# Attention and two feed-forward layers on one core: layer 1's outputs grouped in DRAM, and the refill of the weight slots rescheduled

## The chip, the cores and the metric

The kernel runs on one core of a Trainium2 chip. Its time is the device time of one execution, in microseconds (us); three executions of the kernel before took 1013.91, 1014.51 and 1015.23 us, so the median is 1014.51 us. Less is better.

## The reference

Inputs are float32, the four weight matrices float64.

```python
local = softmax(causal(q @ k.T / 8)) @ v           # 4 batches, 8 heads, 576 rows, 64 columns
mem   = (phi(q) @ M_prev) / (phi(q) @ z_prev)       # phi(x) = x + 1 above 0, exp(x) below
x     = sigmoid(beta) * mem + (1 - sigmoid(beta)) * local     # laid out as 2304 tokens x 512
h = x @ w_in;  x = g1(h) @ w_out                   # layer 1: 512 -> 2048 -> 512
h = x @ w_in2; y = leaky(h, 0.01) @ w_out2         # layer 2, the same sizes
```

`g1(h)` is h above 1, 0 below -1, and (h+1)^2/4 between. Each float32 product is done as three products of a high and a low part, so weights and activations are split in two before TensorE uses them.

## The kernel before

The first 211 us are attention with the first weights; the change leaves them alone. After that come four parts of 36 steps each: layer 1's first half of the 2048 hidden columns (part 0), its second half (part 1), and the same for layer 2 (parts 2 and 3). Tokens go in chunks of 256, nine in all, in groups `(0,1) (2,3) (4,5) (6,7) (8,)`: a pair takes 8 steps, one for each block f of 128 hidden columns, and the single chunk 4 steps with two blocks in each. A step is one run of h (the first product, 12 matmuls of 512 columns for a pair) and one run of Y (the second product) of a block three steps older. Parts 2 and 3 do Y with seven products in place of eight, from sums and differences of weights. h has one PSUM bank only: TensorE can start the next h when ScalarE has copied the last one out.

A part needs 16 weight halves of 512 KB: `in0` to `in7` for h and `o0` to `o7` for Y, each with one slot in SBUF, and in parts 2 and 3 also `ex0` to `ex3` (768 KB, sums for two o halves). They come as float64 bit patterns and are decoded: one ScalarE instruction (L613), five on VectorE (L615 to L623), then the split (L638 and L639).

For parts 1 to 3 the halves are decoded during the part before, each about two steps after the one before (`COUNTS`, L607, 16 in a part's 36 steps), stored to `w_d` in DRAM (L641; the sums to `ex_d`, L678 and L680), and read back into the slots at the part's start. `renew` (L698) issues all these reads, as soon as a slot is free by the plan: `in0` and `in1` four steps before the part's first step, then two a step, the o slots from one step before it on (fetches at L702).

Layer 1's outputs go through DRAM too: part 0 stores sums (`yp_d`), part 1 loads them (`pp`, L876), adds them (L886) and stores y (`y_d`, L880); parts 2 and 3 read y as x (L730). Each of these tiles holds one chunk, so a pair's half of the columns goes in four transfers of 128 KB. Layer 2 keeps its sums in `op_d` with two transfers of 256 KB a chunk, and writes `out` likewise (L955, loads at L848).

The order of every engine's instructions is fixed ahead by a planner (`Plan.order`). Each task has an engine, a cost, a priority in steps, its predecessors and its buffers ("rooms"); the planner plays the engines forward in time and always takes the ready task of lowest priority value. For a DMA it counts 0.6 us on the issuing queue and a constant landing time (`lag`, 4.6 us for the float64 loads, 5.2 for the fetches), whatever else is moving. On the chip every engine then runs its list in order and waits where the data isn't there. All DMAs of the four parts are issued from SyncE's queue (SP), in order.

Of the kernel before, what the change touches and what calls it, by code (L numbers as in the profile page):

```python
# [8 lines left out]
F32 = mybir.dt.float32  # L9
# [124 lines left out]
def attn_moe_moe_kernel(ctx, tc, q, k, v, m_prev, z_prev, beta, w1i, w1o, w2i, w2o, out):  # L134
# [97 lines left out]
    yp_d = [dram.tile([128, 4, TC], F32, name=f"yp_d{c}") for c in range(NCH)]  # L232
    y_d = [dram.tile([128, 4, TC], F32, name=f"y_d{c}") for c in range(NCH)]
    op_d = [{c: dram.tile([128, 2, DM], F32, name=f"op_d{m}_{c}") for c in ([NCH - 1] if m == 0 else range(NCH))} for m in range(2)]
# [372 lines left out]
    PER, AHEAD, DELAY, COUNTS = 36, 3, 4, (17, 17, 14)  # L607
# [76 lines left out]
    HALVES = [(f, 0) for f in range(NSLOT)] + [(f, 1) for f in range(NSLOT)]  # L684

    def weights(seg, k, prio, after, kept, halves):

        f, x = HALVES[k]
        parts = decode(seg, f, x, prio, after)
        if x == 0 or not SEVEN[seg]:  # L690
            kept[f, x] = [keep_half(seg, f, x, *parts, prio)[1]]
            return
        halves.append(parts)
        if f % 2:
            kept[f, x] = kept[f - 1, x] = keep_out(seg, f // 2, *zip(*halves), prio)
            halves.clear()

    def renew(seg, kept):  # L698
        base = PER * seg

        def fetch(room, src, after):
            return steps.add("SP", SEND, prio - 1.5, after, [room], lambda: nc.sync.dma_start(out=as_r(at(room)), in_=src), lag=5.2)  # L702

        for f, x in HALVES:
            free = f // 2 - (1 if x else 4)
            prio, after = base + free - 0.4, [*kept[f, x], mm_at[base + min(free, 0) - 1]]
            room = Room(f"o{f}" if x else f"in{f}")
            ready = fetch(room, w_d[seg][f, x], after)
            if x == 0 or not SEVEN[seg]:
                half_room[seg, f, x], half_ready[seg, f, x] = room, ready  # L710
                continue
            out_room.setdefault((seg, f // 2), []).append(room)
            out_ready.setdefault((seg, f // 2), []).append(ready)
            if f % 2:
                ex = Room(f"ex{f // 2}")
                out_room[seg, f // 2].append(ex)
                out_ready[seg, f // 2].append(fetch(ex, ex_d[seg][f // 2], after))

    def load_x(seg, group, prio):

        room, ready = Room("x"), []
        for j, c in enumerate(group):
            raw = Room("xraw")

            def load(c=c, raw=raw):
                xf = staging(at(raw))
                if SEGS[seg][0] == 0:
                    load_chunk(c, xf)
                else:
                    nc.sync.dma_start(out=xf, in_=y_d[c])  # L730

            after = stored_y.get((seg, c), []) if SEGS[seg][0] else []
# [112 lines left out]
    def load_kept(pp, keep, rows):  # L845
        for i in range(2):
            o = at(pp)[:, i]
            nc.sync.dma_start(out=o.rearrange("p a t -> p (a t)") if rows else o, in_=keep[i])  # L848
# [10 lines left out]
    def finish_plain(seg, group, banks, lhs, after, step):  # L859
        half, pair, n, add = SEGS[seg][1], len(group) == 2, group[0], steps.add  # L860
        for i, lh in enumerate(lhs):
# [3 lines left out]

            t = add("ACT", 2 * from_psum(512), step - 2, after, [*banks.rooms, lh], copies)

            def places(d, i=i):

                if pair:  # L870
                    return [(k, j, d[n + j][:, 2 * i + k]) for k in range(2) for j in range(2)]
                return [(k, None, d[n][:, 2 * k:2 * k + 2]) for k in range(2)]

            def load(pp, places=places):
                for k, j, d in places(yp_d):
                    nc.sync.dma_start(out=at(pp)[:, k] if j is None else at(pp)[:, k, j], in_=d)  # L876

            def store(lh=lh, places=places):
                for k, j, d in places(y_d if half else yp_d):
                    nc.sync.dma_start(out=d, in_=at(lh)[k] if j is None else at(lh)[k][:, j])  # L880

            ts = [t]
            if half:
                pp = Room("pp")
                before = add("SP", 4 * SEND, step - 2, [stored_y[seg - 1, n, i]], [pp], lambda pp=pp, load=load: load(pp), lag=4.0)
# [8 lines left out]
    def finish(seg, group, j, banks, y3, lhs, after, step):  # L894

        layer, half = SEGS[seg][:2]
        pair, n = len(group) == 2, group[0]
        rows = layer == 1 or not pair
        c = n + j
        s, lh, add, tt = Room("s"), lhs[j], steps.add, vec.tensor_tensor  # L900

        def cols(d, i):
            return d[n + i].rearrange("p (b j) t -> p j b t", j=2)[:, j]

        if rows:
            keep = [op_d[layer][c][:, i] for i in range(2)]
        else:
            keep = [cols(yp_d, i) for i in range(2)]
        if half and layer:
            goal = [out[TC * c + 128 * i:TC * c + 128 * i + 128] for i in range(2)]  # L910
        elif half and not rows:
            goal = [cols(y_d, i) for i in range(2)]
        else:
            goal = keep
# [5 lines left out]
        def sums_a():  # L920
            (s0, s1), (lo, hi) = at(s), at(lh)
# [6 lines left out]
        def sums_b():  # L928
            (s0, s1), (lo, hi) = at(s), at(lh)
            tt(lo[:, 1], s1[:, 0], s1[:, 1], ALU.add)  # L930
            tt(lo[:, 0], s1[:, 0], lo[:, 0], ALU.subtract)
# [8 lines left out]
        if half and rows and not layer:  # L940
            return turn_single(lh, t, banks, step)
        if half:
            pp = Room("pp")

            before = add("SP", 2 * SEND, step - 1, [stored_y[seg - 1, c, 0]] if rows else [stored_y[seg - 1, n, i] for i in range(2)], [pp],
                         lambda: load_kept(pp, keep, rows), lag=4.0)
            ts = [add("DVE", dve(512), step, [t, before], [lh, pp], lambda i=i: vec.tensor_tensor(
                at(lh)[i], at(lh)[i], at(pp)[:, i], ALU.add), lag=SLACK) for i in range(2)]
        else:
            ts = [t, t]  # L950

        def store():
            for i in (1, 0):
                o = at(lh)[i]
                nc.sync.dma_start(out=goal[i], in_=o.rearrange("p a t -> p (a t)") if rows else o)  # L955

        t = add("SP", 2 * SEND, step + 0.2, ts, [lh], store, lag=3.0)
        if rows:
            stored_y[seg, c, 0] = stored_y[seg, c, 1] = t
        else:  # L960
            stored_y[seg, n, j] = t
        if half and not layer:
            for i in range(2):
                stored_y.setdefault((seg + 1, n + i), []).append(t)

    def turn_single(lh, t, used, step):

        n, banks, res, pp, add = NCH - 1, Room(used.kind), Room("lh"), Room("pp"), steps.add

        def turn():  # L970
            for i in range(2):
                x = at(lh)[i].rearrange("p a t -> p (a t)")
                for et in range(4):
                    pe.transpose(at(banks)[et // 2][:, et % 2, 128 * i:128 * i + 128], x[:, 128 * et:128 * et + 128], ident)

        def load():
            for i in range(2):
                nc.sync.dma_start(out=at(pp)[:, i], in_=yp_d[n][:, 2 * i:2 * i + 2])

        def store():  # L980
            for i in range(2):
                nc.sync.dma_start(out=y_d[n][:, 2 * i:2 * i + 2], in_=at(res)[i])

        before = add("SP", 2 * SEND, step - 1, [stored_y[0, n, i] for i in range(1)], [pp], load, lag=4.0)
        t = add("PE", 900, step + 1.2, [t], [lh, banks], turn)
        ts = [add("DVE", dve(512), step - 1, [t, before], [banks, res, pp], lambda i=i: vec.tensor_tensor(
            at(res)[i], at(banks)[i], at(pp)[:, i], ALU.add)) for i in range(2)]
        t = add("SP", 2 * SEND, step + 2, ts, [res], store, lag=3.0)
        stored_y.setdefault((2, n), []).append(t)
# [10 lines left out]
    def plan_steps():  # L1000
        step, queue, ready_x, used = 0, [], None, "Yb"
        whens = [PER * (seg + i / n) for seg, n in enumerate(COUNTS) for i in range(n)]
        decodes = [(when, 1 + k // 16, k % 16) for k, when in enumerate(whens)]
        kept, halves = {seg: {} for seg in range(1, 4)}, []
        groups = [(seg, g) for seg in range(4) for g in GROUPS]

        def pop(step):
            seg, group, p, j, gg, ready, banks, (y3, lhs) = queue.pop(0)
            pair, layer = len(group) == 2, SEGS[seg][0]
            if (seg, group) == groups[-1] and p >= NSLOT // 2 - 2:  # L1010
                last_parts.append((p, gg, banks, y3))
                if not last_pp:
                    last_pp.append(Room("pp"))
                    keep = [op_d[1][NCH - 1][:, i] for i in range(2)]
                    steps.add("SP", 2 * SEND, step - 2, [stored_y[2, NCH - 1, 0]], [last_pp[0]], lambda: load_kept(last_pp[0], keep, True))
# [17 lines left out]
        for i, (seg, group) in enumerate(groups):  # L1033
# [12 lines left out]
            for p in range(NSLOT // 2):  # L1046
                gg = Room("gg") if pair or p % 2 == 0 else gg
                g, all_ready = (Room("ga"), Room("gb")), []
                for f in ((2 * p, 2 * p + 1) if pair else (2 * p,)):
# [20 lines left out]
                    while decodes and decodes[0][0] - AHEAD <= step:  # L1070
                        when, n, k = decodes.pop(0)
                        weights(n, k, when + DELAY, [mm], kept[n], halves)
# [4 lines left out]
                    if f == 2 and i + 1 < len(groups):  # L1077
                        ready_x = load_x(*groups[i + 1], step + 1)
# [5 lines left out]
            if i % 5 == 4 and seg < 3:  # L1084
                renew(seg + 1, kept[seg + 1])
# [106 lines left out]
```

## Time and profile before

| | |
|---|---|
| median of three runs | 1014.51 us |
| profiled execution, its own time | 1012.95 us |
| span in the profile | 1011.1 us |
| TensorE busy | 983.5 us (97%) |
| VectorE busy | 719.0 us (71%) |
| ScalarE busy | 596.7 us (59%) |
| DMA moved | 164.36 MB |

In the rows, PE is TensorE, PEld its weight load, DVE VectorE, ACT ScalarE, SP the queue that issues the DMAs. PEclk 1.00 is 2.4 GHz granted, 0.50 is 1.2 GHz. L641 is line 641 of the kernel. A bracket at the end of a row is the idle time before the instruction and what ended it.

### The profile page before, as it was taken

The page shows a single profiled execution, that of the slowest core. Times are in us where ns is not written, and L with a number is a line of the kernel's source. Part 1 is how long each engine was busy: PE and PEld are TensorE (multiplying, and loading weights), DVE is VectorE, ACT ScalarE, POOL GpSimd, SP SyncE. Part 2 cuts the span into 40 slices and gives each one's busy share as a digit, 9 for nine tenths or more (in the row PEclk, how much of TensorE's full clock was granted, in tenths as well). Part 3 has the DMA queues.
Part 4 walks back from the last instruction along what each step waited for, and adds up shares of the span by engine and source line. Part 5 has one row for each costly group of instructions (what it writes and reads, how often), then busy time and mean ns, then how long its engine had stood idle before and what let it go on. Part 6 is the DMA issues. An engine that isn't in the chain of part 4 may idle for free.

```text
span 1011.1 us, 19985 instructions
## 1 busy us (share of the span) xinstructions
PE 983.5 (97%) x7794; PEld 865.7 (86%) x7794; DVE 719.0 (71%) x1571; ACT 596.7 (59%) x1056; POOL 50.7 (5%) x78
## 2 busy tenths in 40 slices
PE   8999999999999999899999998899999999999997
PEld 6888888888888888788888897799999999999997
DVE  7999987758675666556766565697888874665646
ACT  7899888866565666555556563364454643443433
POOL 1332221100000000000000000000000000000000
PEclk9999999999999999999999999899999999999999
DMA  9666743133644339945353589654332993212203
GB/s 195 166 151 151 181 115 91 46 113 111 196 147 168 130 140 310 334 133 185 121 198 135 198 300 391 221 176 151 142 132 100 306 394 94 84 35 70 70 15 104
DMA packets 141661, 164.36 MB, mean 163 GB/s; under 512 B 70016, under 2 KB 110208, under 8 KB 141568
## 3 DMA queue, kind: packets, MB, share of 16 engines
q1 hardware_dynamic: 139696, 162.44, 49.9%
q8 instruction: 61, 1.00, 0.4%
q10 hardware_dynamic: 1872, 0.66, 0.3%
q14 instruction: 32, 0.26, 0.1%
HBM read 108.02 MB, written 55.05 MB: 161 GB/s over the span
## 4 chain that ended last, share of the span: by engine, by line
PE 74%; DVE 11%; DMA 9%; ACT 4%; issue 2%; SPq 0%; DVEq 0%; ACTq 0%
PE h L744 12%; PE h L745 12%; PE h L746 12%; PE Y L746 11%; PE Y L745 11%; PE Y L744 11%; DVE e L395 4%; DMA w_d<-raw 2%; ACT e L400 2%; PE W L291 2%; DMA i<-w_d 2%; DMA raw<-in_moe_w_in_dram 1%; PE W L430 1%; DMA q<-in_q_dram 1%; DMA raw<-y_d 1%
## 5 line engine op out<-in xcount | busy, mean ns | idle before, releaser
L744 PE MATMUL h<-ffn_x,i 128*128 128x512 f32 (+1 forms) x312 | 116.7, 374 | 8.0 <-ACT ga L798 6.2
L744 PE MATMUL h<-xh,i 128*128 128x512 f32 (+1 forms) x320 | 119.1, 372 | 3.2 <-ACT gb L802 3.2
L745 PE MATMUL h<-xl,i 128*128 128x512 f32 (+1 forms) x320 | 118.8, 371 | 0.0
L746 PE MATMUL h<-xh,i 128*128 128x512 f32 (+1 forms) x320 | 118.2, 370 | 0.0
L745 PE MATMUL Y<-gl,o 128*128 128x512 f32 (+1 forms) x320 | 117.8, 368 | 0.0
L744 PE MATMUL Y<-gh,o 128*128 128x512 f32 (+1 forms) x320 | 117.8, 368 | 0.0
L746 PE MATMUL Y<-gh,o 128*128 128x512 f32 (+1 forms) x320 | 117.7, 368 | 0.0
L745 PE MATMUL h<-ffn_x,i 128*128 128x512 f32 (+1 forms) x312 | 116.2, 372 | 0.0
L746 PE MATMUL h<-ffn_x,i 128*128 128x512 f32 (+1 forms) x312 | 115.9, 371 | 0.0
L801 ACT ACTIVATE r<-h 128x512 f32<-128x512 f32 x70 | 41.9, 599 | 116.7 <-PE h L746 116.7
L745 PE MATMUL Y<-o,gh 128*128 128x256 f32 x288 | 81.5, 283 | 0.0
L746 PE MATMUL Y<-o,gl 128*128 128x256 f32 x288 | 81.5, 283 | 0.0
L744 PE MATMUL Y<-o,gh 128*128 128x256 f32 x288 | 81.3, 282 | 0.0
L400 ACT ACTIVATE e<-e,mx 128x384 f32<-128x384 f32 (+4 forms) x144 | 71.7, 576 | 15.8 <-DVE mx L395 15.7
L744 PEld LDWEIGHTS h<-ffn_x,i 128*128 128x128 f32 x312 | 59.5, 191 | 17.9 <-ACT ga L798 6.8
L744 PEld LDWEIGHTS h<-xh,i 128*128 128x128 f32 x320 | 60.8, 190 | 13.1 <-ACT gb L802 3.8
L811 ACT ACTIVATE gh<-gb 128x512 fp32r<-128x512 f32 (+1 forms) x72 | 52.8, 738 | 29.2 <-DVE gb L831 28.4
L746 PEld LDWEIGHTS h<-xh,i 128*128 128x128 f32 x320 | 60.8, 190 | 10.5
L744 PEld LDWEIGHTS Y<-gh,o 128*128 128x128 f32 x320 | 60.3, 189 | 10.1
L745 PEld LDWEIGHTS Y<-gl,o 128*128 128x128 f32 x320 | 60.3, 189 | 10.0
L746 PEld LDWEIGHTS Y<-gh,o 128*128 128x128 f32 x320 | 60.3, 189 | 10.0
L745 PEld LDWEIGHTS h<-xl,i 128*128 128x128 f32 x320 | 60.9, 190 | 8.9
(174 smaller groups left out, 2351.8 us busy)
## 6 DMA issues: line engine op xcount, KB each, us to landing
w_d<-raw SPq DMA_DIRECT2D x48, 512.0 KB, 2.8
raw<-in_moe_w_in_dram SPq DMA_DIRECT2D x32, 512.0 KB, 4.6
raw<-in_moe_w_out_dram SPq DMA_DIRECT2D x32, 512.0 KB, 3.9
i<-w_d SPq DMA_DIRECT2D x24, 512.0 KB, 5.5
o<-w_d SPq DMA_DIRECT2D x24, 512.0 KB, 7.6
raw<-y_d SPq DMA_DIRECT2D x18, 512.0 KB, 3.8
raw<-x_d SPq DMA_DIRECT2D x12, 512.0 KB, 4.1
ex<-ex_d SPq DMA_DIRECT2D x8, 768.0 KB, 8.3
```

The costliest lines, as they stand in the source:

```text
L291: pe.transpose(t[:, c:c + 128], x, ident)
L395: vec.tensor_tensor_reduce(out=out, in0=src, in1=mk, op0=ALU.add, op1=ALU.min, scale=1.0, scalar=3e38, accum_out=at(st)[1][:, col:col + 1])
L400: lambda x=x, w=w, col=col: act.activation(at(x)[:, 0:w], at(x)[:, 0:w], AF.Exp, bias=at(st)[1][:, col:col + 1], scale=-1.0))
L430: pe.matmul(o[r:r + 64, a:a + W1], at(pt)[:, c + r:c + r + 64], x[:, j, h], start=(j == 0), stop=(j == i))
L744: pe.matmul(o, wh, xh, start=first, stop=False)
L745: pe.matmul(o, wh, xl, start=False, stop=False)
L746: pe.matmul(o, wl, xh, start=False, stop=last)
L801: t1 = add("ACT", from_psum(512), prio, [mm], [hp, r], lambda: act.activation(at(r), at(hp), AF.Relu, bias=0.5, scale=0.5))
L811: h = add("ACT", from_sbuf(width * (b - a)), prio + late, after, [x, gg], lambda: act.activation(view(at(gg)[0])[:, a + c:b + c], view(at( ...
```

## The change

Three things change, all in the four parts.

1. `yp_d` and `y_d` become `y_d[0]` and `y_d[1]`, one DRAM tile for a group. The two output buffers `lo` and `hi` become one tile `lh`, so that one transfer of 512 KB stores or loads what took four of 128 KB; in layer 2 one of 512 KB takes the place of two of 256 KB (`op_d`, `out`).
2. Of each part's 16 halves only 12 (`in0` to `in7`, `o0` to `o3`) are decoded early and go through DRAM: from 29 steps before the part, every 2.0 steps. The last four, `o4` to `o7`, are decoded straight into their slots around the part's first steps (their float64 loads are added at steps -1, 1, 2 and 3 of the part). In parts 2 and 3 a new `split_out` makes `ex2` and `ex3` in place as well.
3. `renew` goes. Each slot has a step of its own at which its fetch is added, after the h of that step; the planner's landing time of a fetch is 6.0 us now. The x of the group after a single chunk is asked for one step earlier.

```diff
-    PER, AHEAD, DELAY, COUNTS = 36, 3, 4, (17, 17, 14)
+    PER, AHEAD, DELAY, DIRECT_DELAY = 36, 2, 2, 2
...
+    def split_out(seg, p, raws, ws, ts, prio):
+        rooms, t = [Room(f"o{2 * p}"), Room(f"o{2 * p + 1}"), Room(f"ex{p}")], Room("t")
...
+        t0 = steps.add("DVE", 1340, prio, ts, [wa, wb, t], combos)
+        for i, w in enumerate(ws):
+            t1 = steps.add("ACT", 540, prio, [t0], [w, rooms[i]], ...)
+            ready.append(steps.add("DVE", dve(512), prio, [t1], [w, rooms[i]], ...))
+        t1 = steps.add("ACT", 830, prio, [t0], [t, ex], ...)
+        ready.append(steps.add("DVE", 870, prio, [t1], [t, ex], ...))
...
+    STAGED = [(f, 0) for f in range(NSLOT)] + [(f, 1) for f in range(4)]
+    DECODE = [-29 + 2.0 * k for k in range(len(STAGED))]
+    FILL = (-4, -3, -2, -1, -1, 0, 1, 2), (-1, 0, 2, 3)
+    DIRECT = {4: 1, 5: 2.2, 6: 3.4, 7: 5}
...
+        for (f, x), when in zip(STAGED, DECODE):
+            todo.append((base + when - AHEAD, lambda after, ...: stage(f, x, base + when + DELAY, after)))
+            at_step = FILL[x][f]
+            todo.append((base + at_step, lambda after, ...: fill(f, x, base + a, after)))
+        for f, when in DIRECT.items():
+            todo.append((base + when - AHEAD, lambda after, ...: direct(f, base + when + DIRECT_DELAY, after)))
...
-            t = add("SP", 4 * SEND, step + 0.2, ts, [lh], store, lag=3.0)
+            t = add("SP", SEND, step + 0.2, ts, [lh], lambda lh=lh, place=place: nc.sync.dma_start(
+                out=place(y_d[half]), in_=at(lh)[2]), lag=4.0)
...
-            if i % 5 == 4 and seg < 3:
-                renew(seg + 1, kept[seg + 1])
```

`direct` calls `decode` and then `split_half` (part 1) or, for two halves, `split_out` (parts 2 and 3).

## Rows read from the trace of the kernel before

**Rows 1.** The page: busy us (share of the span) xinstructions of each engine

```profile
PE 983.5 (97%) x7794; PEld 865.7 (86%) x7794; DVE 719.0 (71%) x1571; ACT 596.7 (59%) x1056; POOL 50.7 (5%) x78
```

**Rows 2.** Windows by stretch: us, busy (x instructions) by engine, PEclk, DMA share, GB/s

```profile
400.00:450.00 50.00, 46.80 (x238) 39.71 (x237) 27.78 (x48) 27.80 (x53) 0.00 (x0) 0.97 0.70 245
597.00:655.00 58.00, 50.03 (x299) 44.49 (x298) 34.77 (x63) 24.25 (x42) 0.00 (x0) 0.94 0.87 319
850.00:990.00 140.00, 140.00 (x910) 128.26 (x909) 82.03 (x162) 56.15 (x95) 0.00 (x0) 1.00 0.17 57
990.00:1011.10 21.10, 14.82 (x124) 14.61 (x122) 13.78 (x34) 5.54 (x12) 1.56 (x2) 0.93 0.37 125
```

**Rows 3.** Timeline of TensorE: the h matmuls that began after a wait

```profile
427.25 0.50 PE L744 MATMUL h<-xh,i 128*128 128x512 f32 x1 [2.54 <-ACT gb L802]
...
610.74 0.50 PE L744 MATMUL h<-ffn_x,i 128*128 128x512 f32 x1 [1.00 <-ACT ga L798]
624.41 0.50 PE L744 MATMUL h<-ffn_x,i 128*128 128x512 f32 x1 [2.17 <-ACT ga L798]
632.05 0.50 PE L744 MATMUL h<-ffn_x,i 128*128 128x512 f32 x1 [1.74 <-ACT gb L798]
641.88 0.50 PE L744 MATMUL h<-ffn_x,i 128*128 128x512 f32 x1 [3.06 <-ACT ga L798]
```

**Rows 4.** Windows of 5 us in which the granted clock was below 1.00

```profile
425.00:430.00 5.00, 2.75 (x8) 2.23 (x9) 4.84 (x9) 3.95 (x8) 0.00 (x0) 0.81 0.65 253
430.00:435.00 5.00, 5.00 (x20) 4.00 (x20) 0.88 (x3) 2.24 (x4) 0.00 (x0) 0.85 0.85 257
...
630.00:635.00 5.00, 3.26 (x12) 2.45 (x11) 2.84 (x6) 3.16 (x5) 0.00 (x0) 0.79 1.04 416
635.00:640.00 5.00, 3.81 (x23) 3.29 (x21) 1.20 (x2) 0.00 (x0) 0.00 (x0) 0.87 0.81 307
640.00:645.00 5.00, 3.12 (x10) 2.50 (x11) 3.95 (x8) 2.57 (x5) 0.00 (x0) 0.81 0.71 210
645.00:650.00 5.00, 5.00 (x32) 4.58 (x31) 4.79 (x10) 2.51 (x4) 0.00 (x0) 0.85 0.30 115
```

**Rows 5.** Timeline of ScalarE: the waits ahead of those in group 3

```profile
423.49 0.68 ACT L613 ACTIVATE w<-raw 128x512 f32<-128x512 f32 x1 [4.89 <-DMA raw<-in_moe_w_in_dram]
...
605.15 0.69 ACT L613 ACTIVATE w<-raw 128x512 f32<-128x512 f32 x1 [2.15 <-DMA raw<-in_moe_w_in_dram]
...
620.04 0.85 ACT L811 ACTIVATE gh<-gb 128x768 fp32r<-128x768 f32 x1 [4.99 <-DVE gb L831]
...
630.30 0.60 ACT L864 ACTIVATE lo<-Y 128x512 f32<-128x512 f32 x1 [4.71 <-DMA y_d<-lo]
...
640.66 0.68 ACT L613 ACTIVATE w<-raw 128x512 f32<-128x512 f32 x1 [6.41 <-DMA raw<-in_moe_w_in_dram]
```

**Rows 6.** Chain of waits: transfers at the parts' bounds (start us, us, what)

```profile
416.25 7.22 DMA raw<-in_moe_w_in_dram
...
633.36 7.28 DMA raw<-in_moe_w_in_dram
```

**Rows 7.** DMA issues: line, xcount, KB each, median us from issue to landing

```profile
w_d<-raw SPq DMA_DIRECT2D x48, 512.0 KB, 2.8
...
raw<-in_moe_w_out_dram SPq DMA_DIRECT2D x32, 512.0 KB, 3.9
```

**Rows 8.** Windows: the first 25 us of parts 2 and 3

```profile
600.00:625.00 25.00, 21.83 (x146) 19.86 (x145) 16.06 (x29) 11.05 (x21) 0.00 (x0) 1.00 1.03 380
800.00:825.00 25.00, 25.00 (x170) 23.18 (x169) 22.29 (x49) 14.08 (x26) 0.00 (x0) 1.00 0.98 352
```

**Rows 9.** Lines of VectorE, 211 to 1000 us: busy us, mean ns

```profile
L617 DVE SCALAR_TENSOR_TENSOR da<-w,da 128x512 int32<-128x512 int32 x52 | 35.8, 689 | 2.3 <-ACT w L613 0.6
...
L619 DVE TENSOR_SCALAR dr<-da 128x512 int32<-128x512 int32 x52 | 22.1, 426 | 1.2
```

**Rows 10.** Timeline of VectorE in the tail

```profile
1005.57 0.42 DVE L1102 TENSOR_TENSOR lo<-s 128x256 f32<-128x256 f32 x1 [1.36 <-DMA out_dram<-lo]
```

More of the change, by code (lines that the diff above doesn't have):

```diff
@@ L682, in keep_out @@
         return [*done, steps.add("SP", 3 * SEND, prio + 0.5, [t1], [t, *ws], store, lag=4.5)]
[L684 to L708, printed above, removed]
+    def split_out(seg, p, raws, ws, ts, prio):
+        rooms, t = [Room(f"o{2 * p}"), Room(f"o{2 * p + 1}"), Room(f"ex{p}")], Room("t")
+        out_room[seg, p] = rooms
+        (wa, wb), tt = ws, vec.tensor_tensor
+        def combos():
+            b11, b12, b21, b22 = (at(w)[:, c:c + 256] for w in ws for c in (0, 256))
+            x = at(t)
+            tt(x[:, 1], b22, b12, ALU.subtract)
+            tt(b12, b12, b11, ALU.subtract)
+            tt(x[:, 0], b22, b12, ALU.subtract)
+            tt(x[:, 2], x[:, 0], b21, ALU.subtract)
+        def flat():
+            return at(t).rearrange("p a c -> p (a c)")
+        t0 = steps.add("DVE", 1340, prio, ts, [wa, wb, t], combos)
+        ready = []
+        for i, w in enumerate(ws):
+            t1 = steps.add("ACT", 540, prio, [t0], [w, rooms[i]], lambda i=i, w=w: act.activation(at(rooms[i])[:, 0], at(w), AF.Copy))
+            ready.append(steps.add("DVE", dve(512), prio, [t1], [w, rooms[i]], lambda i=i, w=w: vec.tensor_tensor(
+                at(rooms[i])[:, 1], at(w), as_r(at(rooms[i])[:, 0]), ALU.subtract)))
+        ex = rooms[2]
+        t1 = steps.add("ACT", 830, prio, [t0], [t, ex], lambda: act.activation(at(ex)[:, 0], flat(), AF.Copy))
+        ready.append(steps.add("DVE", 870, prio, [t1], [t, ex], lambda: tt(at(ex)[:, 1], flat(), as_r(at(ex)[:, 0]), ALU.subtract)))
+        out_ready[seg, p] = ready
@@ new lines, in attn_moe_moe_kernel, with weights, stage, direct @@
+    STAGED = [(f, 0) for f in range(NSLOT)] + [(f, 1) for f in range(4)]
+    DECODE = [-29 + 2.0 * k for k in range(len(STAGED))]
+    FILL = (-4, -3, -2, -1, -1, 0, 1, 2), (-1, 0, 2, 3)
+    DIRECT = {4: 1, 5: 2.2, 6: 3.4, 7: 5}
+    def weights(seg):
+        base, kept, halves, todo = PER * seg, {}, [], []
+        def stage(f, x, prio, after):
+            parts = decode(seg, f, x, prio, after)
+            if x == 0 or not SEVEN[seg]:
+                kept[f, x] = [keep_half(seg, f, x, *parts, prio)[1]]
+                return
+            halves.append(parts)
+            if f % 2:
+                kept[f, x] = kept[f - 1, x] = keep_out(seg, f // 2, *zip(*halves), prio)
+                halves.clear()
+        def direct(f, prio, after):
+            parts = decode(seg, f, 1, prio, after)
+            if not SEVEN[seg]:
+                split_half(seg, f, 1, *parts, prio)
+                return
+            halves.append(parts)
+            if f % 2:
+                split_out(seg, f // 2, *zip(*halves), prio)
+                halves.clear()
+        def fetch(room, src, prio, after):
+            return steps.add("SP", SEND, prio, after, [room], lambda: nc.sync.dma_start(out=as_r(at(room)), in_=src), lag=6.0)
+        def fill(f, x, prio, after):
+            room, after = Room(f"o{f}" if x else f"in{f}"), [*after, *kept[f, x]]
+            ready = fetch(room, w_d[seg][f, x], prio, after)
@@ L716, in renew, with load_x @@
                 out_room[seg, f // 2].append(ex)
-                out_ready[seg, f // 2].append(fetch(ex, ex_d[seg][f // 2], after))
-    def load_x(seg, group, prio):
-        room, ready = Room("x"), []
+                out_ready[seg, f // 2].append(fetch(ex, ex_d[seg][f // 2], prio, after))
+        for (f, x), when in zip(STAGED, DECODE):
+            todo.append((base + when - AHEAD, lambda after, f=f, x=x, when=when: stage(f, x, base + when + DELAY, after)))
+            at_step = FILL[x][f]
+            todo.append((base + at_step, lambda after, f=f, x=x, a=at_step: fill(f, x, base + a, after)))
+        for f, when in DIRECT.items():
+            todo.append((base + when - AHEAD, lambda after, f=f, when=when: direct(f, base + when + DIRECT_DELAY, after)))
+        return todo
+    def load_x(seg, group, prio, mm):
+        room, ready, n = Room("x"), [], group[0]
         for j, c in enumerate(group):
@@ L729, in load @@
                 else:
-                    nc.sync.dma_start(out=xf, in_=y_d[c])
-            after = stored_y.get((seg, c), []) if SEGS[seg][0] else []
+                    nc.sync.dma_start(out=xf, in_=y_d[1][n][:, :, c - n])
+            after = [mm, *stored_y.get((seg, c), [])] if SEGS[seg][0] else [mm]
             t = steps.add("SP", SEND * (1 + (SEGS[seg][0] == 0)), prio - 1.5, after, [raw], load, lag=5.2)
@@ L843, in epilogue, with load_kept @@
         return ready
[L845 to L848, printed above, removed]
+    def load_kept(pp, c):
+        nc.sync.dma_start(out=at(pp).rearrange("p i a t -> p i (a t)"), in_=op_d[c])
     def plain(f, y, gg, s, banks, et, pair):
@@ L864, in copies, with place @@
                     act.activation(at(lh)[k], banks()[2 * i + k], AF.Copy)
+            def place(d, i=i):
+                return d[n].rearrange("p k j t -> p (k j) t")[:, 4 * i:4 * i + 4]
             t = add("ACT", 2 * from_psum(512), step - 2, after, [*banks.rooms, lh], copies)
[L868 to L880, printed above, removed]
             ts = [t]
@@ L894, in finish @@
     def finish(seg, group, j, banks, y3, lhs, after, step):
[L896 to L899, printed above, removed]
+        half, pair, c = SEGS[seg][1], len(group) == 2, group[j]
         s, lh, add, tt = Room("s"), lhs[j], steps.add, vec.tensor_tensor
[L902 to L914, printed above, removed]
         def copies():
@@ L939, in finish @@
         t = add("DVE", 2 * dve(256), step - 1.9, [t], [s, lh], sums_b, lag=None if half else SLACK)
-        if half and rows and not layer:
-            return turn_single(lh, t, banks, step)
+        ts, goal = [t, t], op_d[c]
         if half:
-            pp = Room("pp")
-            before = add("SP", 2 * SEND, step - 1, [stored_y[seg - 1, c, 0]] if rows else [stored_y[seg - 1, n, i] for i in range(2)], [pp],
-                         lambda: load_kept(pp, keep, rows), lag=4.0)
+            pp, goal = Room("pp"), out[TC * c:TC * c + TC].rearrange("(i p) m -> p i m", i=2)
+            before = add("SP", SEND, step - 1, [stored_y[seg - 1, c]], [pp], lambda: load_kept(pp, c), lag=4.0)
@@ L962, in finish @@
[L962 to L989, printed above, removed]
@@ L991, in attn_moe_moe_kernel @@
+        stored_y[seg, c] = add("SP", SEND, step + 0.2, ts, [lh], lambda: nc.sync.dma_start(
+            out=goal, in_=at(lh)[2].rearrange("p (i a) t -> p i (a t)", i=2)), lag=4.0)
     class Banks:
@@ L1001, in plan_steps @@
         step, queue, ready_x, used = 0, [], None, "Yb"
-        whens = [PER * (seg + i / n) for seg, n in enumerate(COUNTS) for i in range(n)]
-        decodes = [(when, 1 + k // 16, k % 16) for k, when in enumerate(whens)]
-        kept, halves = {seg: {} for seg in range(1, 4)}, []
+        todo = sorted((t for seg in range(1, 4) for t in weights(seg)), key=lambda t: t[0])
         groups = [(seg, g) for seg in range(4) for g in GROUPS]
@@ L1013, in pop @@
                     last_pp.append(Room("pp"))
-                    keep = [op_d[1][NCH - 1][:, i] for i in range(2)]
-                    steps.add("SP", 2 * SEND, step - 2, [stored_y[2, NCH - 1, 0]], [last_pp[0]], lambda: load_kept(last_pp[0], keep, True))
+                    steps.add("SP", SEND, step - 2, [stored_y[2, NCH - 1]], [last_pp[0]], lambda: load_kept(last_pp[0], NCH - 1))
                 return
@@ L1069, in plan_steps @@
                     mm_at[step] = mm
-                    while decodes and decodes[0][0] - AHEAD <= step:
-                        when, n, k = decodes.pop(0)
-                        weights(n, k, when + DELAY, [mm], kept[n], halves)
+                    while todo and todo[0][0] <= step:
+                        todo.pop(0)[1]([mm])
                     ready = epilogue(seg, group, f, hp, g, gg, step, mm)
@@ L1076, in plan_steps @@
                         queue.append((seg, group, p, f % 2, gg, ready, banks[0], third))
-                    if f == 2 and i + 1 < len(groups):
-                        ready_x = load_x(*groups[i + 1], step + 1)
+                    if f == (2 if pair else 0) and i + 1 < len(groups):
+                        ready_x = load_x(*groups[i + 1], step + pair, mm)
                     if step >= 3:
@@ L1094, in last_sums @@
         s0, s1 = tiles["s"][0]
[L1095 removed]
+        lo, hi = (x.rearrange("p a t -> p (a t)") for x in tiles["lh"][0][0:2])
         act.activation(s0, yp[0], AF.Copy)
@@ L1153, in attn_moe_moe_kernel @@
                  s=[(take("s0", 2, 256), take("s1", 2, 256))],
-                 lh=[[take(f"{t}{i}", 2, 256) for t in ("lo", "hi")] for i in range(2)])
+                 lh=[(t[:, 0:2], t[:, 2:4], t) for t in (take(f"lh{i}", 4, 256) for i in range(2))])
     for f in range(NSLOT):
```

26 lines of the change are left out of this document (7 added, 19 removed).

## The prediction

> **What bounds the kernel now.** I began with the share of each engine: TensorE is busy 97% of the span [rows 1]. The change takes nothing from it and gives it nothing, so all that can be won or lost is the time in which TensorE waits or runs at the lower clock, and I looked for that stretch by stretch. Between the end of attention and 990 us only two stretches have idle TensorE, the bounds from part 0 to 1 and from part 1 to 2: 50.00 - 46.80 = 3.20 us and 58.00 - 50.03 = 7.97 us, 11.17 us together [rows 2]. The bound from part 2 to 3 has none: in 800 to 825 us TensorE is busy throughout [rows 8].
>
> Then the waits one by one. Five h runs make up 10.5 of the 11.17 us [rows 3], and all wait for ScalarE to copy the last h out. ScalarE itself was held [rows 5]: at 423.49 and 640.66 by a float64 load (4.89 and 6.41 us), at 605.15 by another (2.15 us, ahead of the wait at 610.74), at 630.30 by an earlier store of y that had not landed (4.71 us), and at 620.04 by VectorE (4.99 us). So the path is DMA, ScalarE or VectorE, h, TensorE. A wait of ScalarE's costs TensorE less than itself: 4.89 gave 2.54, 4.99 gave 2.17, 4.71 gave 1.74 and 6.41 gave 3.06. The first 2.3 to 3.4 us are hidden behind the Y run.
>
> After three of the waits (2.54, 1.74 and 3.06 us idle) the granted clock falls to 1.2 GHz for a while. A mean of 0.81 and 0.85 over 10 us is (0.19 + 0.15) x 5 / 0.5 = 3.4 us at half speed, which loses 1.7 us of work; 0.79 with 0.87 and 0.81 with 0.85 are the same again [rows 4]. Three falls cost 5.1 us. After 1.00 and 2.17 us idle the clock stayed.
>
> What can be won is thus 11.17 + 5.1 = 16.3 us, and all of it lies at two bounds.
>
> **Why the DMAs are late there.** 600 to 625 us moved 380 GB/s, with the engines occupied 1.03 of the time [rows 8]. Two float64 loads took 7.2 and 7.3 us from issue to landing [rows 6], where the planner counts 4.6 and the median of such loads is 3.9 [rows 7].
>
> **The change, part by part.**
>
> *Bytes.* For each part four halves no longer go through DRAM: four stores and four reads of 512 KB, 4 MB. In parts 2 and 3 two sums of 768 KB go the same way, 3 MB more. In all 12 + 6 = 18 MB of the 164 MB. Each of those stores took 2.8 us in the median [rows 7], and each also held SP's queue until VectorE was done with the half; that leaves the bounds too, since the last early half is now decoded 7 steps before its part.
>
> *What still moves at a bound.* In the first four steps of a part (some 21 us) I count, in units of 512 KB: three in fetches, three o fetches, three float64 loads, two x, three stores of y: 14, or 7.3 MB at part 1. Part 2 has two ex of 768 KB and one kept sum besides: 9.4 MB. Part 3 has the ex alone: 8.9 MB. At 380 GB/s 21 us carry 8.0 MB. So part 1's bound fits, part 2's is over by 1.4 MB or 3.8 us, and part 3's by 0.9 MB or 2.4 us. Steps -4 to -1 have about 0.5 MB each but for the last, and start with no backlog.
>
> The Trainium skill, "DMA: Bandwidth & Descriptors", section Specifications, gives a lower limit for a core's HBM traffic, some 358 GB/s. The row of part 2 shows 380 over 25 us, so the measurement decides here; by 358 the 9.4 MB would end 1.5 us later and the forecast would be about as much slower.
>
> *Direct halves.* Their loads sit in that traffic, and ScalarE's L613 waits for them in its list, ahead of the copies that free h. Part 1: lateness nil to 2 us, below what the Y run hides, so 0. Part 2: the last loads up to 3.8 us late, which by the pairs above is 0.4 to 1.5 us of TensorE for each; I take two at 1.5 and one fall of the clock, 3.0 + 1.7 = 4.7 us. Part 3: up to 2.4 us late, at the edge of what is hidden; I take one wait like that at 610.74, 1.0 us. Bounds: nothing at all on one side; on the other all four loads late in every part, which is a rival below.
>
> *VectorE for the direct halves in parts 2 and 3.* A decode is three instructions of 0.69 us and two of 0.43 [rows 9], 2.9 us. `split_out` has four of 256 columns, which I price at 0.43, two of 512 at 0.69 and one of 768, 0.95 as an estimate between: 4.1 us. Four halves come to 4 x 2.9 + 2 x 4.1 = 19.8 us, due before the last Y block at step 9. Without decoding VectorE is busy 82.03 of 140 us, and 910 matmuls at 33 a step make that stretch 27.6 steps of 5.1 us [rows 2]: 2.1 us are free in a step, 18.9 in nine. This just about fits; those 82 us also hold the closing sums of three pair groups, none of which falls in a part's first nine steps, so there is somewhat more room. I take 0; without that cover it is 0.9 us and more at each of two parts.
>
> *Decoding at 2.0 steps.* It was about 2.1 steps for part 1 and 2 and 2.6 for part 3. In part 2 VectorE gets fuller (it was busy 22.29 of 25 us at 800 us with no wait of TensorE [rows 8]). 0; from below 0, from above a wait of 1 us for each of the four o halves, 4 us.
>
> *Grouped y.* In parts 0 and 1 the pairs' 96 transfers become 24, in layer 2 54 become 27: some 100 fewer issues, and stores that land as one. The wait at 630.30, a buffer still being stored, loses its cause in part: fewer issues stand in front of it. What it saves is inside the 16.3 us. In the tail VectorE waits 1.36 us for the last store of `out` to leave its buffer [rows 10]; one transfer issued a little earlier but twice as large may land some tenths sooner or later: 0, within 0.5.
>
> *x asked for one step earlier; attention, tail.* Unchanged work on engines that have room: 0.
>
> **Sum.** 16.3 removed, 4.7 + 1.0 = 5.7 come back: -10.6 us. From the profiled execution, 1012.95, that is 1002.3. It lies 1.56 below the median of the three runs, so on the median the forecast is 1014.5 - 10.6 = 1003.9 us.
>
> **The rivals.**
>
> *All waits go (0.21).* If loads at part 2 and 3 are late by under 2.3 us, nothing comes back: 1014.5 - 16.3 = 998.2. For it: the 18 MB that go stood at or close to the bounds. Against: 9.4 MB in 21 us.
>
> *Half goes (0.14).* The float64 loads stay late, and only the waits for y's store and for VectorE behind `pp` go: 2.17 + 1.74 and one fall, 5.6 us: 1008.9. For it: three of the five waits follow a float64 load, and the change puts such loads at the bounds still.
>
> *Nothing (0.05).* The fetches could only start when a slot came free, and for the in slots that step is what it was; if the fetches alone fill the DMAs, the waits keep their place: 1014.5 within 2 us. Against: the stores of the last halves and a third of the o fetches' bytes are gone from there.
>
> *Slower: the direct loads hold ScalarE (0.14).* Before, no float64 load stood at the bound of parts 2 and 3, and none waited at 352 GB/s. Now four stand at each of three bounds, just behind the fetches. One held as at 640.66 costs 3.06 + 1.7 = 4.8 us. Up to three of them are paid by the 16.3 us; from the fourth on the change loses. With two at each bound: 6 x 4.8 - 16.3 = +12.5, 1027 us. It decides at a landing over some 8 us after issue.
>
> The Trainium skill, the same page, section "Queues, rings and completion order", says that an engine consumes a queue's descriptors in ring order, and all these come by SP's queue. By that rule a load behind three fetches waits for all three; the two loads of 7.2 and 7.3 us agree. It speaks for this rival, and the sum by it is that rival's.
>
> **How the numbers follow.** The forecast has 0.46, with a range of its own of 1000 to 1007. All waits gone 0.21, half 0.14, nothing 0.05, slower 0.14. The range goes from 997.5 (all gone and some tenths in the tail) to 1012.5, which leaves out the slower case and nothing, under 0.2. What a measurement of this kernel can tell from no change is about 0.2%, 2 us: faster 0.81, same 0.05, slower 0.14.
>
> **What would show it.** Right: idle TensorE at 400 to 450 us gone; at 600 to 650 us two waits or so, behind L613; under 1.5 us idle near 800; about 146 MB moved; no wait of ScalarE's L864 for a store. Wrong: ScalarE waits of over 5 us for a float64 load at 800 us; TensorE's Y waiting for `o` or `ex` (then VectorE was too full); idle TensorE in the middle of a part; or waits at the old places with fewer bytes, which would say that bytes weren't the cause.

## The result, and the profile after

The changed kernel took 996.59 us (median of four runs, 996.44 to 997.11), the kernel before 1014.21 us beside it (1012.18 to 1015.23). The ratio is 0.983, 95% interval 0.9813 to 0.9847: 17.6 us faster, where 10.6 were forecast; the time lies 0.9 us below the stated range. The profiled execution took 997.11 us with a span of 995.3, which is 15.8 us less than the profiled execution before. The other 1.8 us are the choice of executions: before, the profiled one was quicker than its median, after, slower.

Windows of the changed kernel at the three bounds and the tail, columns as in [rows 2]:

```profile
380.00:430.00 50.00, 50.00 (x310) 45.09 (x308) 25.28 (x46) 30.39 (x60) 0.00 (x0) 1.00 0.63 221
590.00:640.00 50.00, 50.00 (x321) 45.58 (x321) 37.02 (x68) 25.25 (x46) 0.00 (x0) 1.00 0.66 243
780.00:830.00 50.00, 49.95 (x328) 45.78 (x328) 44.92 (x92) 26.67 (x47) 0.00 (x0) 1.00 0.77 282
975.00:995.30 20.30, 13.10 (x110) 12.89 (x108) 12.28 (x29) 4.72 (x9) 1.56 (x2) 0.88 0.43 130
```

All that the prediction saw to be won has been won. Of 11.17 us idle at the bounds [rows 2] 0.05 are left, no h waits as those of [rows 3] did, and the granted clock never leaves 1.00 there, where three falls had cost 5.1 us [rows 4].

Parts 2 and 3 begin at 599.0 and 790.3 us here, where they began at 604.0 and 807.2. The first 25 us of each, to be set beside [rows 8] (which begin some us ahead of the parts), and the transfers of the whole page:

```profile
600.00:625.00 25.00, 25.00 (x160) 22.72 (x159) 17.25 (x30) 11.44 (x18) 0.00 (x0) 1.00 1.02 389
790.00:815.00 25.00, 24.95 (x154) 22.25 (x153) 21.05 (x45) 12.78 (x22) 0.00 (x0) 1.00 1.01 384
...
DMA packets 128524, 145.47 MB, mean 146 GB/s; under 512 B 67760, under 2 KB 103344, under 8 KB 128432
```

18.9 MB are gone, as counted. But for these 25 us the DMAs are as full as they were, at part 2 389 GB/s with a share of 1.02 against 380 and 1.03, and TensorE doesn't wait there. So 25 us of full DMAs do not hold it by themselves. What has become shorter is the full stretch; 600 to 640 us before, then in the changed kernel:

```profile
600.00:640.00 40.00, 33.90 (x209) 30.17 (x207) 20.80 (x37) 14.80 (x26) 0.00 (x0) 0.96 1.00 378
600.00:640.00 40.00, 40.00 (x252) 36.25 (x251) 31.83 (x57) 18.46 (x30) 0.00 (x0) 1.00 0.72 271
```

Three of part 2's four waits [rows 3] came after 620 us, late in that stretch. Whether fewer bytes or another order took them away these rows don't tell; the experiments do in part.

The float64 loads there, as SP's queue issued them, and ScalarE's instruction that needs each:

```profile
578.05 11.56 SPq L741 DMA_DIRECT2D i<-w_d  x5
589.66 0.42 SPq L247 DMA_DIRECT2D raw<-in_moe_w_out_dram  x1
597.79 0.32 SPq L741 DMA_DIRECT2D o<-w_d  x1
...
606.99 0.33 SPq L247 DMA_DIRECT2D raw<-in_moe_w_out_dram  x1
...
612.33 0.43 SPq L247 DMA_DIRECT2D raw<-in_moe_w_out_dram  x1
...
618.14 0.33 SPq L247 DMA_DIRECT2D raw<-in_moe_w_out_dram  x1
```

```profile
602.48 0.68 ACT L612 ACTIVATE w<-raw 128x512 f32<-128x512 f32 x1
...
615.50 0.67 ACT L612 ACTIVATE w<-raw 128x512 f32<-128x512 f32 x1 [1.68 <-DMA raw<-in_moe_w_out_dram]
...
622.53 0.66 ACT L612 ACTIVATE w<-raw 128x512 f32<-128x512 f32 x1
...
626.72 0.67 ACT L612 ACTIVATE w<-raw 128x512 f32<-128x512 f32 x1 [1.65 <-DMA raw<-in_moe_w_out_dram]
```

Take the second and the fourth load. They landed 615.50 - 606.99 = 8.5 and 626.72 - 618.14 = 8.6 us after issue: no sooner than the 7.2 and 7.3 us of [rows 6]. What differs is how long before ScalarE's turn they were issued. ScalarE came to them at 615.50 - 1.68 = 613.82, 6.8 us after issue, and at 625.07, 6.9 us after. Before, it came 640.66 - 6.41 - 633.36 = 0.9 and 423.49 - 4.89 - 416.25 = 2.4 us after issue [rows 5, 6]. I call this the lead. A wait is the landing less the lead; with a lead of 6.8 it is 1.7 us, which the Y run hides. The first load went out at 589.66, ahead of the first o fetch, and was there when ScalarE came to it 12.8 us later; the third was there after 10.2 us. The kernel before bears this out with another load:

```profile
596.54 0.39 SPq L245 DMA_DIRECT2D raw<-in_moe_w_in_dram  x1
```

It took 605.15 - 596.54 = 8.6 us as well, but ScalarE came to it at 605.15 - 2.15 = 603.00 [rows 5], a lead of 6.5 us, and so waited 2.15 us and not 6.41.

### The profile page after: what moved, and what is told of

Read it like the earlier page. It is cut to its first block, busy times and chain, and to the rows that moved or that the text cites. A ratio compares the mean times of both kernels' runs of the same rounds, so it can differ in the third digit from the quotient of the medians.

```text
span 995.3 us, 19716 instructions
## 1 busy us (share of the span) xinstructions
PE 977.6 (98%) x7794; PEld 861.8 (87%) x7794; DVE 719.2 (72%) x1567; ACT 597.3 (60%) x1052; POOL 50.7 (5%) x78
## 4 chain that ended last, share of the span: by engine, by line
PE 83%; DVE 10%; ACT 3%; issue 2%; DMA 1%; DVEq 0%; SPq 0%; ACTq 0%
PE h L789 13%; PE h L790 13%; PE h L791 13%; PE Y L791 12%; PE Y L790 12%; PE Y L789 12%; DVE e L394 3%; PE W L290 2%; ACT e L399 2%; PE W L429 2%; PE W L375 1%; DVE qs L346 1%; DVE ph L358 1%; DMA qt<-in_q_dram 1%; PE W L425 1%
## 5 line engine op out<-in xcount | busy, mean ns | idle before, releaser
L789 PE MATMUL h<-ffn_x,i 128*128 128x512 f32 (+1 forms) x312 | 115.2, 369 | 0.0
L790 PE MATMUL h<-ffn_x,i 128*128 128x512 f32 (+1 forms) x312 | 115.0, 369 | 0.0
L791 PE MATMUL h<-ffn_x,i 128*128 128x512 f32 (+1 forms) x312 | 114.6, 367 | 0.0
L850 DVE SCALAR_TENSOR_TENSOR ga<-ga,r 128x512 f32<-128x512 f32 (+1 forms) x40 | 25.5, 639 | 65.7 <-ACT r L848 65.6
L850 DVE SCALAR_TENSOR_TENSOR gb<-gb,r 128x512 f32<-128x512 f32 (+1 forms) x40 | 25.5, 638 | 59.0 <-ACT r L848 59.0
```

What stands on the lines that cost most here:

```text
L789: pe.matmul(o, wh, xh, start=first, stop=False)
L790: pe.matmul(o, wh, xl, start=False, stop=False)
L791: pe.matmul(o, wl, xh, start=False, stop=last)
L850: new.append(add("DVE", dve(512 if pair else 256), prio, [t, t1], [g[k], r], lambda k=k: vec.scalar_tensor_tensor(out=fresh(k), in0=fresh( ...
```

## The experiments

Two theories stood at the start. The issue theory: a float64 load holds ScalarE because SP's list, which runs in order, reaches it late. The bytes theory: the bounds carry more than the DMAs can move in time. The list theory, which e9, e10 and e13 were made to test, is the first one widened: a load is late by all that stands ahead of it in SP's list, fetches that wait for a slot among it. Each kernel was timed against the kernel before, whose median in these sessions was 1013.0 to 1014.7 us; a difference between two changed kernels comes from different sessions, and one under some 2 us is not certain. Idle TensorE below is that of the four parts in a profiled execution.

**The two halves of the change.** e1 has the new tiles and transfers for y alone, e2 the new schedule of the weights alone:

```diff
 # e1: on the kernel before
+    y_d = [{g[0]: dram.tile([128, 4, len(g), TC], F32, ...) for g in GROUPS} for m in range(2)]
...
 # e2: on the changed kernel
+    yp_d = [dram.tile([128, 4, TC], F32, ...) for c in range(NCH)]
+    y_d = [dram.tile([128, 4, TC], F32, ...) for c in range(NCH)]
```

> The kernel before with the first part of the change alone: y and the kept sums in group tiles, one transfer for four; weights as before. Issue theory (a float64 load holds ScalarE because SyncE's in-order list reaches it late, behind stores that wait for VectorE and buffers that wait for stores to land): the stores of decoded halves stay in the list, so the waits on float64 loads stay and only those behind y go: idle TensorE from 211 us to the end of part 3 falls from 11.2 us to 5 to 9 us, 1006 to 1011 us. Bytes theory (the bounds carry too many bytes for the DMAs): the bytes are the same, 1011 to 1015 us.

Measured: 1013.01 us, ratio 0.9985 (0.9974 to 0.9996), 12.8 us idle.

> The changed kernel with y in four transfers of 128 KB a half as before; the new schedule of the weights alone. Issue theory: nearly all waits go, since the stores of decoded halves have left the bounds, 997 to 1002 us. Bytes theory: as many bytes as in the changed kernel, 996 to 999 us. If the grouping of y were what mattered: over 1006 us.

Measured: 995.59 us, ratio 0.981 (0.9793 to 0.9826), nothing idle. The grouping of y gives 1.5 us by itself (0.4 to 2.6) and nothing that shows on top of the new schedule; the kernel without it has the lower median by 1.0 us. The whole gain comes with the schedule alone, and the issue theory as I had it is wrong on e1.

**No direct halves; fetches early or by steps.** e3 sends all 16 halves through DRAM, but keeps the fetches by steps. e7 is e3 with the fetches at the steps of the kernel before. e6 is the changed kernel with early fetches and direct halves.

```diff
 # e3
+    STAGED = [(f, 0) for f in range(NSLOT)] + [(f, 1) for f in range(NSLOT)]
+    DECODE = [-36 + 36 / 17 * k for k in range(len(STAGED))]
+    FILL = (-4, -3, -2, -1, -1, 0, 1, 2), (-1, 0, 2, 3, 3, 4, 5, 6)
+    DIRECT = {}
 # e7, on e3; fetch priority 1.9 steps sooner, lag=5.2
+    FILL = (-4, -4, -3, -3, -2, -2, -1, -1), (-1, -1, 0, 0, 1, 1, 2, 2)
 # e6, on the changed kernel
+    FILL = (-4, -4, -3, -3, -2, -2, -1, -1), (-1, -1, 0, 0)
```

> The changed kernel with all 16 halves of a part decoded early and sent through DRAM (one each 36/17 steps, as before), none directly; fetches of o4 to o7 at steps 3 to 6; grouped y stays. Issue theory: stores of decoded halves stand in SyncE's list at the bounds again, so ScalarE waits for float64 loads over 3 us again: 1002 to 1010 us. Bytes theory: the 18 MB are back, 1006 to 1014 us. If spreading the fetches over the steps did it: under 999 us.

Measured: 1000.79 us, ratio 0.9862 (0.9847 to 0.9876), 3.6 us idle, with 164.35 MB moved. None of the three ranges has it.

> As e3_all_staged (all 16 halves through DRAM), but with the fetches at the steps, the priority and the planned landing of the kernel before: what is left of the change is the grouped y and stores planned two steps sooner. If the fetches' steps gave most of e3's gain: 1008 to 1014 us. If the stores' time or the grouping gave it: 999 to 1004 us.

Measured: 1012.21 us, ratio 0.9976 (0.9965 to 0.9988), 12.1 us idle.

> The changed kernel with each fetch added at the step in which its slot comes free (in halves two a step from step -4, o halves at -1 and 0) in place of a step of its own; direct halves stay. If the step of the fetches matters: the first steps' burst comes earlier, float64 loads of the direct halves land later or sooner by 1 to 3 us, waits of 1 to 5 us come back: 998 to 1003 us. If bytes alone matter: 996 to 997 us. Issue theory: 996 to 998 us, since no store that waits for VectorE stands at the bounds.

Measured: 1007.36 us, ratio 0.9925 (0.9905 to 0.9945), 6.8 us idle, slower than any of the three ranges.

The four make a table:

| | fetches early | fetches by steps | gain by steps |
|---|---|---|---|
| all through DRAM | 1012.21 (e7) | 1000.79 (e3) | 11.4 |
| four halves direct | 1007.36 (e6) | 996.59 (changed) | 10.8 |
| gain by direct halves | 4.9 | 4.2 | |

The steps of the fetches (in e7 with their priority and planned landing) are worth over twice as much as the direct halves, with as many bytes, and the two add up. The page of e3 shows that the bytes hadn't gone:

```profile
DMA packets 134284, 164.35 MB, mean 164 GB/s; under 512 B 68400, under 2 KB 104496, under 8 KB 134192
```

**Stores from another queue.** e8 takes the stores that wait for VectorE out of SP's list.

```diff
 # e8: on the kernel before, L641; L678 and L680 likewise
-        return low, steps.add("SP", SEND, prio + 0.5, [t], [raw], lambda: nc.sync.dma_start(...))
+        return low, steps.add("POOL", SEND, prio + 0.5, [t], [raw], lambda: nc.gpsimd.dma_start(...))
```

> The kernel before with the stores of decoded halves and sums (w_d, ex_d) issued from GpSimd's queue in place of SyncE's; nothing else. Issue theory: SyncE no longer stands behind stores that wait for VectorE, so float64 loads go out in time: idle TensorE falls from 11.2 to under 6 us, 1000 to 1008 us. Bytes theory: no change, 1012 to 1016 us.

Measured: 1010.98 us, ratio 0.9965 (0.9954 to 0.9975), 8.6 us idle. That is 3.6 us, less than the issue theory asked for and more than the bytes theory. How much the stores in the list cost it doesn't tell, since another wait grew. A stored half keeps its `raw` buffer, of which there are two, until its store has landed, and the next float64 load stands in SP's list until then. From 380 to 655 us SP waited so for loads of `w_in`, before and then in e8 (us in total, times, longest):

```profile
SPq L245 <- DMA w_d<-raw: 22.3, 8, 5.5
SPq L245 <- DMA w_d<-raw: 43.1, 9, 10.6
```

The load issued at 633.36 in the kernel before was one of them. A direct half isn't stored, and in the changed kernel SP has no such wait from 590 to 640 us, where e3 has 9.3 us of it. So the 4 to 5 us of the direct halves are bytes, stores in the list and this wait together; no run takes them apart.

**Where a load stands in the list.** In the list of e6 the first direct load of part 2 comes behind eight in fetches, `ex0`, two o fetches, `pp` and a store of y; in the changed kernel it comes ahead of the first o fetch. The issues of e6 and ScalarE's wait show what that does:

```profile
598.10 0.32 SPq L741 DMA_DIRECT2D o<-w_d  x1
598.51 0.62 SPq L917 DMA_DIRECT2D pp<-y_d  x1
599.18 0.44 SPq L921 DMA_DIRECT2D y_d<-lh  x1
599.71 0.40 SPq L741 DMA_DIRECT2D o<-w_d  x1
600.16 0.46 SPq L247 DMA_DIRECT2D raw<-in_moe_w_out_dram  x1
```

```profile
611.24 0.67 ACT L612 ACTIVATE w<-raw 128x512 f32<-128x512 f32 x1 [7.23 <-DMA raw<-in_moe_w_out_dram]
```

The load is issued 10.5 us later than in the changed kernel (589.66), behind fetches that wait for their slots, and it lands after 11.1 us, with all that has just been issued in front of it. The lead is 611.24 - 7.23 - 600.16 = 3.9 us. So e9 leaves the early fetches and adds the direct loads 1.5 steps sooner; e10 leaves the fetches by steps and adds the loads a step later.

```diff
 # e9, on e6; e10, on the changed kernel, has "when - 1"; the load's priority moves with it
-            todo.append((base + when - AHEAD, lambda after, ...: direct(...)))
+            todo.append((base + when - 3.5, lambda after, ...: direct(...)))
```

> As e6_early_fetch (fetches as soon as the slot comes free), but each direct float64 load is added 1.5 steps sooner, so that in SyncE's list it stands ahead of the o fetches that wait for their slots. Same bytes, same fetch steps. List theory (what a float64 load has ahead of it in SyncE's list decides: fetches waiting for a slot and the bytes right ahead): most of the 10.8 us between e6 and the changed kernel comes back, 996 to 1001 us. Burst theory (the early fetches fill the DMAs, wherever the loads stand): 1004 to 1008 us.

Measured: 1000.76 us, ratio 0.987 (0.9847 to 0.9893), 2.5 us idle.

> The changed kernel with each direct float64 load added one step later, so that it stands behind o fetches, pp and y's store in SyncE's list; fetch steps unchanged. List theory: waits of ScalarE for these loads of 3 to 7 us, 1000 to 1008 us. Burst theory: the fetches are still spread, 996 to 999 us.

Measured: 1001.34 us, ratio 0.9879 (0.9856 to 0.9902), 2.7 us idle. Its longest wait of ScalarE for such a load is 4.4 us. Moving only the loads gives back 6.6 of the 10.8 us in one direction and costs 4.7 in the other. The list theory holds for most of it. Of the 4 us that e9 still lacks 2.5 are idle TensorE. Its longest wait, 7.3 us, is for the second load of part 2: only the first (590.94) went ahead of the o fetches, while the second, issued at 600.84, still stands behind `ex0`, two o fetches, `pp` and stores of y, with a lead of 2.7 us. What else is in the 4 us is open.

**Bytes ahead and bytes behind.** e4, e5 and e13 add 24 transfers of 512 KB from DRAM to DRAM, eight at each bound; their data is used nowhere. In e4 they share two targets, so that some wait for an earlier one; in e5 each has its own. In both, two stand ahead of each direct load. In e13 all eight stand behind the last one and a store of y.

```diff
 # e4 and e5, ahead of each direct load
+            for i in range(2):
+                steps.add("SP", SEND, prio - 2.1, after, [], lambda i=i: nc.sync.dma_start(out=junk[...], in_=w1o[...]), lag=6.0)
 # e13: after the load of o7, eight of them, added after that load
+            if f == 7:
+                for g in range(4, 8):
+                    extra(g, prio - 1.9, [*after, *loads])
```

> The changed kernel with two extra transfers of 512 KB from DRAM to DRAM (their data is used nowhere) issued just ahead of each of the 12 direct float64 loads: 12 MB more at the three bounds, with no store that waits for VectorE. Bytes theory: waits like those of the kernel before come back, 8 us idle and more, 1007 to 1014 us. Issue theory: the loads land some 3 us later, ScalarE waits 2 to 5 us for some, of which the first 2.3 are hidden: 0 to 5 us idle, 997 to 1003 us.

Measured: 1019.07 us, ratio 1.0038 (1.0024 to 1.0053), 16.9 us idle.

> As e4_bytes_back, but each extra transfer writes a DRAM tile of its own, so none waits for an earlier one and SyncE's list isn't held. Bytes theory: the 12 MB alone bring the waits back: idle TensorE 10 us and more, over 1008 us. Issue theory: what made e4_bytes_back slow was the list held by extra transfers that waited for one another; here the float64 loads are issued in time, land some 3 us later, and cost 0 to 5 us: 996 to 1002 us.

Measured: 1018.83 us, ratio 1.0048 (1.0029 to 1.0067), 15.6 us idle. The two agree, so waits among the extra transfers explain nothing, and at that point the bytes theory looked right. But the extra transfers also change the list: in e5 the first load of part 2 goes out at 603.58, behind an o fetch, `pp` and a store of y, with a lead of 4.0 us. So e5 has more bytes and later loads at once.

> As e5_bytes_no_wait, the same 12 MB of extra transfers into tiles of their own, but all eight of a bound stand behind its last direct float64 load in SyncE's list (and behind one y store) in place of two ahead of each load. List theory: nothing urgent stands behind them for some steps but two loads of the next part's first halves, so most of the 22 us goes: 996 to 1003 us. Bytes theory (so many bytes at a bound cost what they cost): over 1010 us.

Measured: 1000.71 us, ratio 0.9875 (0.9853 to 0.9897), 2.1 us idle. The waits of TensorE in the four parts, e5 first, then e13 (what waited for what: us in total, times, longest):

```profile
PE h L796 <- ACT gb L850: 6.1, 5, 2.5
PE h L796 <- ACT ga L850: 5.7, 3, 3.0
PE h L796 <- ACT ga L854: 2.0, 1, 2.0
PE Y L796 <- ACT lh L959: 1.6, 1, 1.6
PE h L796 <- ACT gb L854: 0.2, 1, 0.2
```

```profile
PE h L801 <- ACT ga L859: 2.1, 1, 2.1
```

```profile
DMA packets 129292, 158.05 MB, mean 158 GB/s; under 512 B 68144, under 2 KB 103728, under 8 KB 128816
```

The same 158.05 MB cost 22.2 us ahead of the loads and 4.1 us behind them. At part 2 the DMAs of e13 are full for 35 us and TensorE doesn't wait:

```profile
605.00:640.00 35.00, 35.00 (x227) 31.99 (x226) 28.15 (x50) 17.13 (x27) 0.00 (x0) 1.00 1.04 395
```

Its one wait of TensorE, 2.1 us, follows a load that stands right behind the extra transfers, at part 1:

```profile
421.41 5.76 SPq L727 DMA_DIRECT2D junk<-in_moe_w_out_dram  x8
430.17 5.25 SPq L246 DMA_DIRECT2D raw<-in_moe_w_in_dram  x2
...
440.53 0.67 ACT L617 ACTIVATE w<-raw 128x512 f32<-128x512 f32 x1 [4.16 <-DMA raw<-in_moe_w_in_dram]
```

That load took 10.4 us; in the changed kernel the one issued at 430.67 landed after 3.8. With the lower clock after it (a mean of 0.71 and 0.95 in the 10 us from 440, 1.7 us of work) the wait is 3.8 of the 4.1 us. This decides against the bytes theory as a sum for the bound: what an urgent load has ahead of it counts. In one queue that runs in order, behind is also later, so e13 does not part the place in the list from the time of the traffic.

**The tail.** The one stretch that became slower is the tail: VectorE waits 2.04 us for the last store of `out`, where it waited 1.36 [rows 10]. One store of 512 KB now holds the whole buffer; the same wait is 2.02 us with the grouping alone (e1) and 1.24 without it (e2). TensorE's idle time at the end went from 6.28 us (from 990 us on [rows 2]) to 7.20 (from 975 us on, the last of the first rows shown after the change).

```profile
989.53 0.43 DVE L1071 TENSOR_TENSOR lh<-s 128x256 f32<-128x256 f32 x1 [2.04 <-DMA out_dram<-lh]
```

e11 (on the changed kernel) and e12 (on e2) put the closing sums into the other output buffer:

```diff
 # e11; e12 likewise
-        lo, hi = (x.rearrange("p a t -> p (a t)") for x in tiles["lh"][0][0:2])
+        lo, hi = (x.rearrange("p a t -> p (a t)") for x in tiles["lh"][1][0:2])
```

> The changed kernel with the closing sums in the other of the two output buffers (its store has long landed), so that VectorE doesn't wait 2.04 us for the last 512 KB store of out. If that wait is on the path to the end: 994.3 to 995.2 us, 1.4 to 2.0 us less than the changed kernel. If another operand is as late: no change, 996.3 to 997 us.

Measured: 995.59 us, ratio 0.9819 (0.9792 to 0.9846), 1.0 us less than the changed kernel, a smaller gain than I expected. The wait is gone, and part of it comes back at the next instructions, where `pp` is now the last to arrive:

```profile
987.58 0.42 DVE L1071 TENSOR_TENSOR lh<-s 128x256 f32<-128x256 f32 x1
988.41 0.42 DVE L1073 TENSOR_TENSOR s<-s,pp 128x256 f32<-128x256 f32 x1 [0.42 <-DMA pp<-op_d]
```

> e2_weights_only (the new schedule of the weights, y in four transfers) with the closing sums in the other output buffer. There the wait in the tail is 1.24 us: 994.2 to 995.0 us if it is on the path, 995.4 to 995.8 us if not.

Measured: 994.98 us, ratio 0.9816 (0.9793 to 0.9839), the lowest median of all, 1.6 us under that of the changed kernel and, with its interval, faster than the kernel before by 16 to 21 us. Its own step over e2 is 0.6 us, with runs from 994.70 to 995.85, so that this last step is not clear of the scatter.

## Why the prediction was wrong in size

*What bounds the kernel* was right: the two bounds, the path through ScalarE to h, the clock's falls, and 16.3 us as all there is. The profiled executions differ by 15.8 us: 11.1 us idle and 5.1 us of clock, less 0.9 in the tail, within 0.5 us. Idle TensorE in the middle of a part, Y waiting for `o` or `ex`, VectorE too full for the direct halves in parts 2 and 3, decoding at 2.0 steps: none of it showed, as forecast.

*Direct halves* is the step that failed, the 5.7 us that were to come back. I had the landing right: 3.8 us over the planned 4.6 make 8.4, and 8.5 and 8.6 were measured. I then took lateness against the planner's figure for ScalarE's wait. The wait is counted from ScalarE's turn, which came 6.8 us after the issue, so 1.7 us were left and nothing reached TensorE. The 5.7 us, with the 1.8 us of the choice of executions and less 0.9 in the tail, are 6.6 of the 7.0 us between forecast and result.

*What still moves at a bound* was counted right and was the wrong measure. The 9.4 MB were there (389 GB/s over 25 us are 9.7), but e13 against e5 shows that the amount by itself says little. From the same error I gave the steps of the fetches no price of their own, although they are some 60% of the gain (10.8 of 17.6 us), and put the 18 MB in the first place; the direct halves, with all that goes with them, are worth 4.2 us.

*Grouped y* was rightly given nothing of its own, and the tail, put at 0 within 0.5, cost 0.9.

*The rivals.* "All waits go", at 998.2, is what happened, but not by its condition as it stands: counted against the planner's 4.6 us the loads were late by 3.8 us and more, and only ScalarE's waits (1.7 us) stayed under 2.3. For the same reason the sign of "slower", a landing over some 8 us after issue, was there (8.5 and 8.6 us) and nothing was lost. The rule of the Trainium skill on ring order ("DMA: Bandwidth & Descriptors", section "Queues, rings and completion order") was the better guide of the two I weighed: e5 and e13 agree with it, 22.2 against 4.1 us for the same transfers ahead of and behind the loads. I read it as speaking for the slower case. The loads did land late behind what was ahead of them, but the lead of some 6.8 us paid for that. The slower case is real, though: e5, with 12 MB more ahead of the loads, is at 1018.8.

## What to carry to other kernels

For a transfer that an engine waits for, compare two times: from its issue to its landing, and from its issue to the engine's turn. When the queue is full, look at what stands ahead of it in the issuing engine's list, above all fetches that wait for a slot, before counting bytes; putting off fetches that nobody needs yet gained 11 us here at the same traffic. See too whether a load waits for its own buffer, because what was in it is still being stored. After a change at one bound read the tail again: the merged store held its whole buffer, and VectorE waited 2.04 us for it in place of 1.36.

## What the runs showed that I had not expected

A stretch of 25 us at 389 GB/s with the DMAs occupied 1.02 of the time cost TensorE nothing, and in e13 neither did one of 35 us at 395 GB/s. And 12 MB of extra transfers, some 30 us of full DMA at that rate, cost 22 us or 4 us by their place in one queue, in e5 together with the later issue of the loads.
